# DMA transposes for the second parity's normalised rows, and attention units with scores and weighted values side by side

## The chip, the core and the metric

The kernel runs on one core of a Trainium2 chip. The metric is the device time of one execution in microseconds, of which medians of several executions are quoted. Each execution comes with the mean clock that was granted to TensorE, as a share of full speed. An execution is called slow when it lies more than 1.5% above the fastest one of the same kernel; the others, fast. Engine names in profile lines: PE is TensorE (matmuls), PEld its weight loads, DVE is VectorE, ACT is ScalarE, POOL is GpSimd, SPq is the queue of SyncE, which issues most DMAs.

## The reference, cut to what matters

```python
xn = layernorm(x)                       # x: 1 x 2048 x 512, bf16
# A: sliding attention, 32 heads of 16, window of 8 keys at distance 2
qkv = xn @ wqkv
s   = softmax(q . k[pos - 0, 2, ..., 14] * scale) @ v  @ wo
# B: MLP with shifted groups
h   = gelu(layernorm(xn) @ w1);  x1 = xn + shift(h) @ w2
g   = silu(x1 + gelu(layernorm(x1) @ w3) @ w4)
out = x + s * g
```

Keys stand at even distances, so even and odd rows never attend to each other. The kernel splits the 2048 rows by parity: chunks 0 and 1 (512 rows each) are the even rows, chunks 2 and 3 the odd ones, the "second parity".

## The kernel before

Each chunk of normalised rows is used transposed (in PE's profile lines `qk_ps<-xnT` and `w_ps<-xn2T`), once as it is (`xnT`, for queries, keys and values) and once normalised again, that is scaled by one factor per row (`xn2T`, for w1). Before the change PE transposes the rows with an identity matrix, a further matmul (`rrep_ps`) spreads the row factors over all partitions, and VectorE multiplies.

```python
def transposes(c, h):                 # h: half of the chunk, 8 PE transposes
    ...
    pin(nc.tensor.transpose(pt[:, dt, j, :], x_c[:, jj, dt * P : (dt + 1) * P], ident[:]))
    ...
    pin(nc.vector.tensor_copy(out=xnT[p][:, :, t0 : t0 + 2 * P], in_=...))

def rr_spread(c):
    ...                               # diagonal of row factors, on VectorE
    pin(nc.tensor.matmul(rp, lhsT=ones_bf[:], rhs=dg, start=True, stop=True))
    nc.scalar.activation(rrep, rp, AF.Copy)

def stage_b(c):                       # w2, residual, third layer norm
    ...
    pin(nc.sync.dma_start(out=x1n_dram[c * CH : (c + 1) * CH, :]..., in_=xn3))
    x1nT = sm4.tile([P, ND, CH], BF16, name="x1nT", tag="s4")
    pin(nc.sync.dma_start_transpose(out=x1nT, in_=x1n_dram[c * CH : (c + 1) * CH, :]))

def fill_mask(p, w):                  # 8 DMAs of 128 KB: mask rows next to each head's keys or queries
    t = (kT[p], qT[p])[w]
    for e in range(2):
        for gr in range(4):
            r = 32 * gr + DH * (1 - e)
            pin(nc.sync.dma_start(out=t[e][r : r + DH, :, :], in_=mask_d[w]....to_broadcast([DH, ND, M])))
```

`pin` keeps an engine's instructions in the order of the program. All pinned `nc.sync` DMAs therefore form one fixed list on SyncE. A stage is named after what it multiplies with (qk, w1, w3) or is stage B. The stages of the first half run in this order:

```python
for c in range(1, NCH):               # before the change
    if c + 1 < NCH: ln_stats(c + 1)
    stage_tr(c); stage_w1(c - 1); rr_spread(c); rr_mult(c)
    if c + 1 < NCH: ln_norm(c + 1); stage_qk(c)
    if c == 2: fill_mask(0, 0); fill_mask(0, 1)
    if c == 1: build_mask()           # rows computed on GpSimd, written to mask_d
stage_b(0); stage_w1(3); stage_b(1); stage_qk(3); stage_b(2)
stage_w3(0); stage_b(3); stage_w3(1); stage_w3(2); stage_w3(3)
```

The second half has 18 attention units. While ScalarE takes exponentials of one unit's scores, PE does pieces of the w4 and wo products ("fill" in the code, not to be confused with the mask fills):

```python
for n, (p, u) in enumerate(order):    # before the change
    prs = [scores(p, u, 0)]
    for f in fill[n][0]: f()
    prs.append(scores(p, u, 1))
    for f in fill[n][1]: f()
    if prev is not None: weighted(*prev)     # 32 matmuls, then VectorE empties the bank
    prev = (p, u, va, prs)
    if n + 1 < len(order): va = values(*order[n + 1])
    ...
```

The softmax here doesn't subtract the row's maximum and nothing guards it: scores larger than these inputs give would overflow.

Of the kernel before, what the change touches and what calls it, by code (L numbers as in the profile page):

```python
# [8 lines left out]
AF = mybir.ActivationFunctionType  # L9
# [6 lines left out]
def kernel(  # L16
# [62 lines left out]
    mask_d = dram.tile([2, 16, M], BF16, name="mask_d")  # L79
    x1n_dram = dram.tile([S, D], BF16, name="x1n_dram")  # L80

    def bigt(shape, name):
        return big.tile(shape, BF16, name=name, tag="big")

    def midt(shape, name):
        return mid.tile(shape, BF16, name=name, tag="s11")
# [30 lines left out]
    def pin(ins):  # L117

        prev = pinned.get(ins.ins.engine)
        if prev is not None:  # L120
            tc.add_manual_dep(
                ins.ins, prev, mybir.DependencyInfo(mybir.DependencyClass.NoSync, mybir.DependencyReason.DATA),
                reason="pinned",
            )
        pinned[ins.ins.engine] = ins.ins.name
        return tc.keep_in_program_order(ins)
# [4 lines left out]
    for c in range(NCH):  # L131
# [14 lines left out]
    nc.sync.dma_start(out=w2_sb, in_=B_w2.rearrange("(g q) n -> q g n", q=P))  # L146
    w3_sb = midt([P, ND, F], "w3_sb")
    nc.sync.dma_start(out=w3_sb, in_=B_w3.rearrange("(dt q) f -> q dt f", q=P))
    wv_sb = const.tile([P, ND, D], BF16, name="wv_sb")
    nc.sync.dma_start(out=wv_sb, in_=wqkv_v[:, :, 2 * D : 3 * D])  # L150
    w4_sb = midt([P, NF, D], "w4_sb")
    nc.sync.dma_start(
        out=w4_sb[:, 0 : NF - 1, :],
        in_=B_w4[0 : (NF - 1) * P, :].rearrange("(ft q) n -> q ft n", q=P),
    )
    nc.sync.dma_start(out=w4_sb[0:FL, NF - 1, :], in_=B_w4[(NF - 1) * P : F, :])
    nc.scalar.preload_act_table_set("gelu_apprx_tanh_and_others")


# [74 lines left out]
    def fill_mask(p, w):  # L234
# [3 lines that stand above are left out]
# [4 lines left out]
                    )  # L242
                )


    NV = 2
    v_aug = []
# [81 lines left out]
    def stage_tr(c):  # L329
        for h in range(TPC // 2):  # L330
            transposes(c, h)

    def rr_spread(c):
        p, k = c // 2, c % 2
# [133 lines left out]
    def w4_tile(c, jj, tag=None):  # L468

        p, i = c // 2, (c % 2) * TPC + jj  # L470
        st = {}

        def half(lo, hi):
            if lo == 0:
                st["pt"] = pst(tag or "w", "w4_ps")[:, 0, :]
            pt = st["pt"]
            for ft in range(lo, hi):
                fs = P if ft < NF - 1 else FL
                pin(
                    nc.tensor.matmul(  # L480
                        pt, lhsT=h3[c][:fs, ft, jj * P : (jj + 1) * P], rhs=w4_sb[:fs, ft, :],
                        start=(ft == 0), stop=(ft == NF - 1),
                    )
                )
            if hi == NF:
                x_i = xn[p][:, i, :]
                pin(nc.vector.tensor_tensor(out=x_i, in0=pt, in1=x_i, op=ALU.add))  # L487
                if tag is not None:
                    nc.scalar.activation(x_i, x_i, AF.Silu)
                else:  # L490
                    st["sig"] = fin.tile([P, D], BF16, name="sig", tag="f")
                    nc.scalar.activation(st["sig"], x_i, AF.Tanh, scale=0.5)

        def gate():

            x_i = xn[p][:, i, :]
            pin(
                nc.vector.scalar_tensor_tensor(
                    out=x_i, in0=st["sig"], scalar=1.0, in1=x_i, op0=ALU.add, op1=ALU.mult
                )  # L500
            )

        return half, gate


# [3 lines left out]
    def values(p, u):  # L509
        q0, nq, k0, nk = units[u]  # L510
        va = v_aug[cnt["v"] % NV]
        cnt["v"] += 1
        vp = pst("b", "v_ps")[:, 0, :]
        for dt in range(ND):
            pin(
                nc.tensor.matmul(  # L516
                    vp[:nk, :], lhsT=xnT[p][:, dt, k0 : k0 + nk], rhs=wv_sb[:, dt, :],
                    start=(dt == 0), stop=(dt == ND - 1),
                )
            )  # L520
        pin(nc.vector.tensor_copy(  # L521
            out=va[:nk, :, 0:DH], in_=vp[:nk, :].rearrange("p (h d) -> p h d", d=DH)
        ))
        return va

    def scores(p, u, dd):
        q0, nq, k0, nk = units[u]
        pr = sm4.tile([P, H * P // 2], BF16, name="prob", tag="s4")
        prv = pr[:, 0 : H * nq // 2].rearrange("p (r x) -> p r x", r=4)
        for h in range(2):  # L530
            st = pst("st"[h], "s_ps")
            for i in range(4):
                dt, e = 2 * dd + i // 2, i % 2
                for b in range(2):
                    r = 64 * h + 32 * b
                    pin(
                        nc.tensor.matmul(  # L537
                            st[:nk, b, i * nq : (i + 1) * nq], lhsT=kT[p][e][r : r + 32, dt, k0 : k0 + nk],
                            rhs=qT[p][e][r : r + 32, dt, q0 : q0 + nq], start=True, stop=True,
                            tile_position=(r, 0),  # L540
                        )
                    )
            with tc.issue_after(last["gelu"].ins):
                nc.scalar.activation(  # L544
                    prv[:nk, 2 * h : 2 * h + 2], st[:nk, :, 0 : 4 * nq], AF.Exp, scale=SCALE
                )
        return pr

    def weighted(p, u, va, prs, tag="o"):
        q0, nq, k0, nk = units[u]  # L550
        r = next(i for i, x in enumerate(runs[p]) if u < x[1])
        ra = runs[p][r][2]
        if u == runs[p][r][0]:
            rw = runs[p][r][3]
            orw[p] = orwp.tile([P, 2 * ND * RW], BF16, name="orw", tag="orw")[:, 0 : 2 * ND * rw].rearrange(
                "p (j s q) -> p j s q", j=2, s=ND
            )
        op = pst(tag, "o_ps")
        for jj in range(2):
            for dt in range(ND):  # L560
                for cg in range(4):
                    b, e = cg // 2, cg % 2
                    pi = jj * 8 + b * 4 + (dt % 2) * 2 + e
                    pin(
                        nc.tensor.matmul(  # L565
                            op[32 * cg : 32 * cg + 32, jj, dt * nq : (dt + 1) * nq],
                            lhsT=va[:nk, dt * 8 + 4 * jj + cg, :],
                            rhs=prs[dt // 2][:nk, pi * nq : (pi + 1) * nq],
                            start=True, stop=True, tile_position=(0, 32 * cg),
                        )  # L570
                    )
        pin(nc.vector.tensor_copy(  # L572
            out=orw[p][:, :, :, q0 - ra : q0 - ra + nq],
            in_=op[:, :, 0 : 4 * nq].rearrange("p j (s q) -> p j s q", q=nq),
        ))
        if u == runs[p][r][1] - 1:
            normalise(p, r)
# [136 lines left out]
    rr_mult(0)  # L714
    ln_norm(1)
    stage_qk(0, [1, 2, 3])
    for c in range(1, NCH):
        if c + 1 < NCH:
            ln_stats(c + 1)
        stage_tr(c)  # L720
        stage_w1(c - 1)
        rr_spread(c)
        rr_mult(c)
        if c + 1 < NCH:
            ln_norm(c + 1)
            stage_qk(c)
        if c == 2:
            fill_mask(0, 0)
            fill_mask(0, 1)
        if c == 1:  # L730
            build_mask()
    stage_b(0)
    stage_w1(3)
    stage_b(1)
# [16 lines left out]
    for n in range(2 * NU):  # L751
        if n < 10:
            t, a, b, c = n, 0, 8, NF
        elif n < 14:
            t, a, b, c = (n // 2 + 5, 0, 4, 5) if n % 2 == 0 else (n // 2 + 5, 5, 9, NF)
        else:
            t, (a, b, c) = NW - 1, ((0, 3, 3), (3, 6, 6), (6, 9, 9), (9, NF, NF))[n - 14]
        fill[n][0].append(lambda t=t, a=a, b=b: w4s[t][0](a, b))
        if c > b:
            fill[n][1].append(lambda t=t, b=b, c=c: w4s[t][0](b, c))  # L760
            if c == NF:
                fill[n + 1][0].append(w4s[t][1])
        if n >= 10:
            fill[n][0].append(lambda i=n - 10: final_tile(0, i))
        if n >= 12 and n % 2 == 0:
            fill[n][2].append(lambda i=n - 12: store(nc.sync, 0, i))
# [16 lines left out]
    for n, (p, u) in enumerate(order):  # L783
        prs = [scores(p, u, 0)]
        for f in fill[n][0]:
            f()
        prs.append(scores(p, u, 1))
        for f in fill[n][1]:
            f()
        if prev is not None:  # L790
            weighted(*prev)
        prev = (p, u, va, prs)
        if n + 1 < len(order):
            va = values(*order[n + 1])
        for f in fill[n][2]:
            f()
# [4 lines left out]
            ident.rearrange("k (h a) -> k a h", a=DH).unsqueeze(3).to_broadcast([P, DH, 8, DH]), AF.Copy,  # L801
        )
    )
    weighted(*prev, tag="s")
    final_tile(1, 0, tag="b")
    final_tile(1, 1, tag="o")
    w4s[NW - 1][1]()
# [48 lines left out]
```

## Time and profile before

| | before |
|---|---|
| median of the first 3 runs | 214.15 us (213.87 to 214.18) |
| span in the profile | 211.9 us |
| PE busy | 201.7 us, 95% |
| next busiest engine, ACT | 139.6 us, 66% |
| mean granted clock | 0.999 |

These are lines of the first page of the profile of the kernel before: busy time by engine, then PE's busy tenths, the granted clock and the DMA share in 40 equal slices of the span.

```profile
PE 201.7 (95%) x1978; PEld 96.5 (46%) x2007; DVE 131.0 (62%) x254; ACT 139.6 (66%) x160; POOL 55.5 (26%) x118
PE   8998999999999999999989999999999999998991
PEclk9999999999999999999999999999999999999999
DMA  5999314998240275599930003724325542445142
```

PE has no hole in its row: a digit of 8 or 9 in every slice but the last. So I took the time for the length of PE's list, and work taken off it for worth its full length unless something new makes PE wait: an estimate from this row, which e10 below bears out (1.5 to 2.6 us gained for 2.2 us taken off).

The next lines are PE's timeline before, in the columns start, length (us), engine, source line, operation, output and inputs, shapes and count. They are the transposes and replication matmuls of chunks 2 and 3, and the first matmuls that read stage B's transposed rows.

```profile
28.35 1.06 PE L321 MATMUL tr_ps<-ident,xn_96 128*128 128x128 bf16 x16
32.70 0.39 PE L348 MATMUL rrep_ps<-xn2T,ones_bf 128*128 128x512 bf16 x1
39.83 1.06 PE L321 MATMUL tr_ps<-ident,xn_96 128*128 128x128 bf16 x16
44.18 0.38 PE L348 MATMUL rrep_ps<-xn2T,ones_bf 128*128 128x512 bf16 x1
65.11 5.13 PE L458 MATMUL w_ps<-x1nT,w_sb 128*128 128x512 bf16 x23
```

From each start to the next matmul's start is 0.89, 0.23, 0.90 and 0.22 us: 2.2 us in all. The w3 stage starts at 65.11 and does not wait.

SyncE's list before, in the same columns (length is now the time to issue, not to land):

```profile
29.59 0.38 SPq L232 DMA_DIRECT2D mask_d<-m_rows_424  x1
35.46 1.74 SPq L240 DMA_DIRECT2D kT_151<-mask_d  x4
44.29 3.58 SPq L240 DMA_DIRECT2D qT_156<-mask_d  x4
55.02 0.40 SPq L436 DMA_DIRECT2D x1n_dram<-xn_662  x1
57.97 2.09 SPq L441 DMA_TRANSPOSE x1nT<-x1n_dram  x1
```

The mask fills are issued from 35.5 to 47.9 us (12.4 us) and, by the DMA share in windows of 1 us, their data flow from 37 to 52. Stage B's first write is issued at 55.0, when the fills are through. Its transpose follows 2.95 us later and lands about 4 us after that, some 3 us before PE needs it.

### The profile page before, as it was taken

Reading aid. Unit: us, or ns where it says so; the run is one execution under the profiler, and the core shown is the slowest. Engines: PE = TensorE matmul, PEld = TensorE weight load, DVE = VectorE, ACT = ScalarE, POOL = GpSimd, SP = SyncE. Lnnn points to the kernel's source line nnn. Section 1 sums busy time; section 2 is a strip of 40 time slices with the busy share of each in tenths; the row PEclk is TensorE's granted clock in tenths of the full one; section 3 lists DMA queues with packets and bytes.
Section 4 is the critical chain, followed back from the end, with each engine's and each line's share of the span. In section 5 each row is a group of like instructions: output and inputs, shape, how many; then the busy total and the mean of one; then the engine's idle time right before and its main releaser. Section 6 shows DMA issues by size and latency. Waiting matters only on the chain.

```text
span 211.9 us, 4839 instructions
## 1 busy us (share of the span) xinstructions
PE 201.7 (95%) x1978; PEld 96.5 (46%) x2007; DVE 131.0 (62%) x254; ACT 139.6 (66%) x160; POOL 55.5 (26%) x118
## 2 busy tenths in 40 slices
PE   8998999999999999999989999999999999998991
PEld 2544454544444444444444444444445544454440
DVE  6879396338839456000014666767767889688785
ACT  2098797943393625565599888788597888975310
POOL 4645774001120202000000008508039070253000
PEclk9999999999999999999999999999999999999999
DMA  5999314998240275599930003724325542445142
GB/s 152 375 395 389 117 8 6 147 145 108 99 99 3 99 198 99 140 174 126 120 39 3 0 3 61 216 80 76 114 82 141 168 103 33 129 121 107 31 147 99
DMA packets 30990, 25.16 MB, mean 119 GB/s; under 512 B 15960, under 2 KB 26424, under 8 KB 30968
## 3 DMA queue, kind: packets, MB, share of 16 engines
q1 hardware_dynamic: 27224, 19.02, 40.0%
q0 software_dynamic: 2192, 4.57, 9.1%
q10 hardware_dynamic: 1552, 1.27, 2.0%
q8 instruction: 16, 0.26, 0.6%
q14 instruction: 6, 0.05, 0.1%
HBM read 16.15 MB, written 4.37 MB: 97 GB/s over the span
## 4 chain that ended last, share of the span: by engine, by line
PE 80%; DVE 7%; DMA 5%; ACT 2%; issue 2%; POOL 1%; SPq 1%; DVEq 0%; ACTq 0%
PE w_ps L458 18%; PE w_ps L480 16%; PE qk_ps L372 10%; PE v_ps L516 7%; PE s_ps L537 7%; PE w_ps L421 6%; PE wo_ps L677 6%; PE w_ps L391 5%; PE o_ps L565 4%; DMA xn_95<-in_A_x_dram 3%; DMA oT_2427<-orw 2%; ACT prob L544 2%; DVE l1s_243 L284 1%; DVE l1s_299 L284 1%; DVE sg L686 1%
## 5 line engine op out<-in xcount | busy, mean ns | idle before, releaser
L544 ACT ACTIVATE prob<-s_ps 128x960 bf16<-128x960 f32 (+2 forms) x72 | 62.7, 925 | 11.6 <-PE s_ps L537 11.2
L480 PE MATMUL w_ps<-w_sb,h3T 128*128 128x512 bf16 (+1 forms) x174 | 43.6, 381 | 0.2 <-issue 0.2
L458 PE MATMUL w_ps<-x1nT,w_sb 128*128 128x512 bf16 (+1 forms) x173 | 38.2, 379 | 0.2
L464 ACT ACTIVATE h3T<-w_ps 128x1024 bf16<-128x1024 f32 x20 | 20.5, 1024 | 20.9 <-PE w_ps L458 20.9
L599 POOL DMA_DIRECT2D oT_1480<-orw x24 | 12.4, 525 | 61.3 <-DVE orw L572 61.3
L458 PEld LDWEIGHTS <-w_sb 128*128 128x128 bf16 (+1 forms) x176 | 17.6, 100 | 20.4
L480 PEld LDWEIGHTS <-h3T 128*128 128x128 bf16 (+1 forms) x176 | 14.7, 98 | 16.4
L521 DVE CAST v_aug_145<-v_ps 128x512 bf16<-128x512 f32 (+1 forms) x9 | 6.1, 681 | 23.1 <-PE v_ps L516 23.0
L572 DVE CAST orw<-o_ps 128x960 bf16<-128x960 f32 (+2 forms) x18 | 19.7, 1097 | 0.4 <-PE o_ps L565 0.4
L372 PEld LDWEIGHTS <-wqk_sb 128*128 128x128 bf16 x136 | 13.3, 98 | 14.3 <-issue 0.3
L599 POOL DMA_DIRECT2D oT_2427<-orw x20 | 10.1, 513 | 20.9 <-DVE orw L572 20.9
L487 DVE TENSOR_TENSOR xn_95<-w_ps,xn_95 128x512 bf16<-128x512 f32 x8 | 5.5, 692 | 16.0 <-PE w_ps L480 16.0
L372 PE MATMUL qk_ps<-xnT_149,wqk_sb 128*128 128x512 bf16 (+1 forms) x71 | 14.3, 355 | 0.3 <-DVE xnT_149 L324 0.2
L391 PE MATMUL w_ps<-xn2T,w_sb 128*128 128x512 bf16 x61 | 14.3, 379 | 0.2
L372 PE MATMUL qk_ps<-xnT_150,wqk_sb 128*128 128x512 bf16 x64 | 14.1, 379 | 0.0
L262 POOL TENSOR_SCALAR l3r<-l3m 128x4 f32<-128x4 f32 x4 | 1.0, 246 | 43.4 <-DVE l3m L270 43.4
L380 ACT ACTIVATE qT_155<-qk_ps 128x1024 bf16<-128x1024 f32 x4 | 4.1, 1030 | 9.8 <-PE qk_ps L372 9.8
L427 DVE TENSOR_TENSOR xn_96<-w_ps,xn_96 128x1024 bf16<-128x1024 f32 x4 | 4.9, 1216 | 8.3 <-PE w_ps L421 8.3
L421 PE MATMUL w_ps<-w_sb,hT_160 128*128 128x512 bf16 x32 | 9.5, 379 | 0.0
L516 PE MATMUL v_ps<-wv_sb,xnT_150 128*128 128x512 bf16 (+1 forms) x28 | 8.9, 383 | 0.4
L391 PEld LDWEIGHTS <-w_sb 128*128 128x128 bf16 x64 | 6.1, 98 | 6.8
L421 PE MATMUL w_ps<-w_sb,hT_159 128*128 128x512 bf16 x30 | 9.1, 379 | 0.1
(161 smaller groups left out, 328.8 us busy)
## 6 DMA issues: line engine op xcount, KB each, us to landing
w_sb<-in_B_w_dram SPq DMA_DIRECT2D x1, 1376.0 KB
w_sb<-in_B_w_dram SPq DMA_DIRECT2D x1, 1280.0 KB
wqk_sb<-in_A_wqkv_dram SPq DMA_DIRECT2D x2, 512.0 KB
w_sb<-in_B_w_dram SPq DMA_DIRECT2D x2, 512.0 KB
xn_96<-in_A_x_dram SPq DMA_DIRECT2D x4, 256.0 KB
xo_1598<-in_A_x_dram POOLq DMA_DIRECT2D x4, 256.0 KB, 3.9
xo_2228<-in_A_x_dram POOLq DMA_DIRECT2D x4, 256.0 KB, 3.7
out_dram<-xo_1598 SPq DMA_DIRECT2D x3, 256.0 KB
```

The costliest lines, as they stand in the source:

```text
L372: nc.tensor.matmul(pt[:, b, h : h + n], lhsT=wqk_sb[:, dt, nt * P : (nt + 1) * P], rhs=xnT[p][:, dt, k * CH + h : k * CH + h + n], start=( ...
L391: nc.tensor.matmul(pt[:, b, :], lhsT=w1_sb[:, dt, g * P : (g + 1) * P], rhs=xn2T[:, dt, :], start=(dt == 0), stop=(dt == ND - 1),)
L421: nc.tensor.matmul(pt[:, j, :], lhsT=w2_src(p, g, m0), rhs=w2_sb[:, g, :], start=(g == 0), stop=(g == ND - 1),)
L458: nc.tensor.matmul(pt[:fs, ft % 2, :], lhsT=w3_sb[:, dt, ft * P : ft * P + fs], rhs=x1nT[:, dt, :], start=(dt == 0), stop=(dt == ND - 1),)
L464: last["gelu"] = nc.scalar.activation(h3T[:, 2 * a : 2 * a + 2, :], pt, AF.Gelu_apprx_tanh)
L480: nc.tensor.matmul(pt, lhsT=h3[c][:fs, ft, jj * P : (jj + 1) * P], rhs=w4_sb[:fs, ft, :], start=(ft == 0), stop=(ft == NF - 1),)
L516: nc.tensor.matmul(vp[:nk, :], lhsT=xnT[p][:, dt, k0 : k0 + nk], rhs=wv_sb[:, dt, :], start=(dt == 0), stop=(dt == ND - 1),)
L537: nc.tensor.matmul(st[:nk, b, i * nq : (i + 1) * nq], lhsT=kT[p][e][r : r + 32, dt, k0 : k0 + nk], rhs=qT[p][e][r : r + 32, dt, q0 : q0 + ...
L544: nc.scalar.activation(prv[:nk, 2 * h : 2 * h + 2], st[:nk, :, 0 : 4 * nq], AF.Exp, scale=SCALE)
L572: pin(nc.vector.tensor_copy(out=orw[p][:, :, :, q0 - ra : q0 - ra + nq], in_=op[:, :, 0 : 4 * nq].rearrange("p j (s q) -> p j s q", q=nq),))
L599: (nc.scalar if (p, r) == (1, 2) and jj else nc.gpsimd).dma_start(out=oT[p][DH * hh : DH * (hh + 1), :, ra : ra + rw], in_=orw[p][32 * cg ...
L677: nc.tensor.matmul(pt, lhsT=oT[p][:, dt, i * P : (i + 1) * P], rhs=wo["sb"][:, dt, lo:hi], start=(dt == 0), stop=(dt == ND - 1),)
```

## The change

Chunks 2 and 3 are no longer transposed by PE. The rows and the scaled rows are written to DRAM and come back through two DMA transposes. To keep the DMA queues free for that, the loads of wv and w4 move behind chunk 2's transposes, and the mask is built behind chunk 3's. In the attention units the weighted values follow directly on the second scores, so that the form of the matmuls changes less often (128\*128, 32\*128 or 128\*32 in the profile lines), and w4 work of units 10 to 13 moves in front of the second scores. The exponentials are pinned to program order. The diff, cut to its core:

```diff
+    def late_loads():                     # wv and w4, until now loaded at the start
+        pin(nc.sync.dma_start(out=late["wv"], in_=wqkv_v[:, :, 2 * D : 3 * D]))
+        pin(nc.sync.dma_start(out=late["w4"][:, 0 : NF - 1, :], in_=B_w4...))
+        ...
+    def dma_tr(c):
+        pin(nc.sync.dma_start(out=xn_dram[0, cs, :]..., in_=x_c))
+        xn2 = sm4.tile([P, TPC, D], BF16, name="xn2", tag="s4")
+        for j in range(TPC):
+            pin(nc.vector.tensor_scalar(out=xn2[:, j, :], in0=x_c[:, j, :], scalar1=r2[:, j : j + 1], ...))
+        pin(nc.sync.dma_start(out=xn_dram[1, cs, :]..., in_=xn2))
+        pin(nc.sync.dma_start_transpose(out=xnT[p][:, :, cs], in_=xn_dram[0, cs, :]))
+        xn2Ts[c] = sm4.tile([P, ND, CH], BF16, name="xn2T", tag="s4")
+        pin(nc.sync.dma_start_transpose(out=xn2Ts[c], in_=xn_dram[1, cs, :]))
...
-    for c in range(1, NCH):  (the loop shown above)
+    ln_stats(2); stage_tr(1); stage_w1(0); rr_spread(1); ln_norm(2)
+    dma_tr(2)
+    late_loads()
+    rr_mult(1); stage_qk(1); ln_stats(3); ln_norm(3)
+    dma_tr(3)
+    build_mask()
+    stage_w1(1); stage_qk(2)
+    fill_mask(0, 0)
+    fill_mask(0, 1)
+    stage_w1(2)
     stage_b(0)
...
-            t, a, b, c = (n // 2 + 5, 0, 4, 5) if n % 2 == 0 else (n // 2 + 5, 5, 9, NF)
+            t, a, b, c = (n // 2 + 5, 0, 5, 5) if n % 2 == 0 else (n // 2 + 5, 5, NF, NF)
...
         prs.append(scores(p, u, 1))
+        if prev is not None:
+            op = weighted(*prev)
         for f in fill[n][1]:
             f()
         if prev is not None:
-            weighted(*prev)
+            keep(*prev[0:2], op)
```

More of the change, by code (lines that the diff above doesn't have):

```diff
@@ L80 @@
     x1n_dram = dram.tile([S, D], BF16, name="x1n_dram")
+    xn_dram = dram.tile([2, M, D], BF16, name="xn_dram")
     def bigt(shape, name):
@@ L148 @@
     nc.sync.dma_start(out=w3_sb, in_=B_w3.rearrange("(dt q) f -> q dt f", q=P))
-    wv_sb = const.tile([P, ND, D], BF16, name="wv_sb")
-    nc.sync.dma_start(out=wv_sb, in_=wqkv_v[:, :, 2 * D : 3 * D])
-    w4_sb = midt([P, NF, D], "w4_sb")
-    nc.sync.dma_start(
-        out=w4_sb[:, 0 : NF - 1, :],
-        in_=B_w4[0 : (NF - 1) * P, :].rearrange("(ft q) n -> q ft n", q=P),
-    )
-    nc.sync.dma_start(out=w4_sb[0:FL, NF - 1, :], in_=B_w4[(NF - 1) * P : F, :])
     nc.scalar.preload_act_table_set("gelu_apprx_tanh_and_others")
@@ L243, in fill_mask @@
                 )
+    late = {}
+    def late_loads():
+        late["wv"] = const.tile([P, ND, D], BF16, name="wv_sb")
+        pin(nc.sync.dma_start(out=late["wv"], in_=wqkv_v[:, :, 2 * D : 3 * D]))
+        late["w4"] = midt([P, NF, D], "w4_sb")
+        pin(
+            nc.sync.dma_start(
+                out=late["w4"][:, 0 : NF - 1, :],
+                in_=B_w4[0 : (NF - 1) * P, :].rearrange("(ft q) n -> q ft n", q=P),
+            )
+        )
+        pin(nc.sync.dma_start(out=late["w4"][0:FL, NF - 1, :], in_=B_w4[(NF - 1) * P : F, :]))
     NV = 2
@@ L331, in stage_tr @@
             transposes(c, h)
+    def dma_tr(c):
+        p, k = c // 2, c % 2
+        cs = slice(k * CH, (k + 1) * CH)
+        x_c = xn[p][:, k * TPC : (k + 1) * TPC, :]
+        pin(nc.sync.dma_start(out=xn_dram[0, cs, :].rearrange("(i q) d -> q i d", q=P), in_=x_c))
+        r2 = r2s.pop(c)
+        xn2 = sm4.tile([P, TPC, D], BF16, name="xn2", tag="s4")
+        for j in range(TPC):
+            pin(
+                nc.vector.tensor_scalar(
+                    out=xn2[:, j, :], in0=x_c[:, j, :], scalar1=r2[:, j : j + 1], scalar2=None, op0=ALU.mult
+                )
+            )
+        pin(nc.sync.dma_start(out=xn_dram[1, cs, :].rearrange("(i q) d -> q i d", q=P), in_=xn2))
+        pin(nc.sync.dma_start_transpose(out=xnT[p][:, :, cs], in_=xn_dram[0, cs, :]))
+        xn2Ts[c] = sm4.tile([P, ND, CH], BF16, name="xn2T", tag="s4")
+        pin(nc.sync.dma_start_transpose(out=xn2Ts[c], in_=xn_dram[1, cs, :]))
     def rr_spread(c):
@@ L480, in half @@
                     nc.tensor.matmul(
-                        pt, lhsT=h3[c][:fs, ft, jj * P : (jj + 1) * P], rhs=w4_sb[:fs, ft, :],
+                        pt, lhsT=h3[c][:fs, ft, jj * P : (jj + 1) * P], rhs=late["w4"][:fs, ft, :],
                         start=(ft == 0), stop=(ft == NF - 1),
@@ L491, in half @@
                     st["sig"] = fin.tile([P, D], BF16, name="sig", tag="f")
-                    nc.scalar.activation(st["sig"], x_i, AF.Tanh, scale=0.5)
+                    pin(nc.scalar.activation(st["sig"], x_i, AF.Tanh, scale=0.5))
         def gate():
@@ L516, in values @@
                 nc.tensor.matmul(
-                    vp[:nk, :], lhsT=xnT[p][:, dt, k0 : k0 + nk], rhs=wv_sb[:, dt, :],
+                    vp[:nk, :], lhsT=xnT[p][:, dt, k0 : k0 + nk], rhs=late["wv"][:, dt, :],
                     start=(dt == 0), stop=(dt == ND - 1),
@@ L543, in scores @@
             with tc.issue_after(last["gelu"].ins):
-                nc.scalar.activation(
+                pin(nc.scalar.activation(
                     prv[:nk, 2 * h : 2 * h + 2], st[:nk, :, 0 : 4 * nq], AF.Exp, scale=SCALE
-                )
+                ))
         return pr
@@ L551, in weighted @@
         r = next(i for i, x in enumerate(runs[p]) if u < x[1])
-        ra = runs[p][r][2]
         if u == runs[p][r][0]:
@@ L571, in weighted, with keep @@
                     )
+        return op
+    def keep(p, u, op):
+        q0, nq, k0, nk = units[u]
+        r = next(i for i, x in enumerate(runs[p]) if u < x[1])
+        ra = runs[p][r][2]
         pin(nc.vector.tensor_copy(
@@ L716 @@
     stage_qk(0, [1, 2, 3])
-    for c in range(1, NCH):
-        if c + 1 < NCH:
-            ln_stats(c + 1)
-        stage_tr(c)
-        stage_w1(c - 1)
-        rr_spread(c)
-        rr_mult(c)
-        if c + 1 < NCH:
-            ln_norm(c + 1)
-            stage_qk(c)
-        if c == 2:
-            fill_mask(0, 0)
-            fill_mask(0, 1)
-        if c == 1:
-            build_mask()
+    ln_stats(2)
+    stage_tr(1)
+    stage_w1(0)
+    rr_spread(1)
+    ln_norm(2)
+    dma_tr(2)
+    late_loads()
+    rr_mult(1)
+    stage_qk(1)
+    ln_stats(3)
+    ln_norm(3)
+    dma_tr(3)
+    build_mask()
+    stage_w1(1)
+    stage_qk(2)
+    fill_mask(0, 0)
+    fill_mask(0, 1)
+    stage_w1(2)
     stage_b(0)
@@ L758 @@
         fill[n][0].append(lambda t=t, a=a, b=b: w4s[t][0](a, b))
+        if b == NF and n < 14:
+            fill[n + 1][0].append(w4s[t][1])
         if c > b:
@@ L803 @@
     )
-    weighted(*prev, tag="s")
+    keep(*prev[0:2], weighted(*prev, tag="s"))
     final_tile(1, 0, tag="b")
```

## The prediction

The sum reads 214.15 - 2.2 - 1.3 + 7 = 217.65, about 218 us. The 1.3 us is my estimate from the 0.11 us of excess in the trace. The 7 us rests on the order of SyncE's list and on my estimate that the write's data come behind the fills'.

> **What bounds the kernel now.** The page's engine table has PE busy 201.7 of 211.9 us (95%), the next engine (ACT) 66%; the chain of waits is 80% PE. From 30 to 110 us PE is busy 9.3 to 10 of every 10. So time taken from PE's in-order list counts, and so does every wait put into it.
>
> **What is removed from PE.**
> (a) Sixteen transposes and one replication matmul for each of the two chunks of the second parity. In PE's timeline transposes take 28.35-29.24 and 39.83-40.73, replication matmuls 32.70-32.93 and 44.18-44.40: 2.2 us in all.
> (b) A steady attention unit takes 4.94 us in six blocks: scores 0.34, eight w4 matmuls 1.84, scores 0.51, three w4 0.75, weighted 0.53, values 0.97. A 512-column matmul costs 0.216, so each full-array block leaves about 0.11 us of excess where the array form changes. [...] Weighted next to scores makes five changes of six in some 13 units, though ACT (84% busy) limits the last four of them. I estimate 1.3 us.
> Together -3.5 us: without a new wait, 210.6 us.
>
> **What is added and moved.** SyncE's queue gets, in fixed order: two 512 KB writes and two transposes for chunk 2, the late weight loads (1.9 MB), the same four for chunk 3, mask rows, sixteen mask fills, and only then stage B's first write and transpose. [...] Durations from the trace: write to usable 2.4-2.9 us, transpose issue 2.1, landing about 4, mask rows to first fill 5.1-5.9, fills 12.4 to issue and about 16 to land, loads about 390 GB/s.
> - Chunk 2: normalised about 22.5 us, transposes landed by about 32. The plain one lands about 29.5, wanted at 31.8: no wait.
> - Chunk 3: normalised about 31; its writes queue behind the late loads (data until about 36), so its transposes issue at 38-43 and land by 45; wanted at 45.6: just in time.
> - Masks: rows cannot go before about 42, fills run about 47-64 (before: 35.5-52). The table's buffer may come later, giving 5 us more.
> - Stage B chunk 0: its write, ready at about 53, sits behind the fills until 60, its data behind theirs until 65; its transpose lands about 70. PE wants it for the first w3 stage at 65.1-2.2 = 62.9. **New wait of about 7 us (3 at best, 12 at worst), all critical.** Before, it landed 3 us early.
>
> Later stages shift whole; the second mask fill has 40 us of slack; the tail is unchanged.
>
> **Prediction:** 214.15 - 2.2 - 1.3 + 7 = about 218 us, slower. Range 209 to 223; the low end is the case in which the masks go out earlier and nothing waits. Chances: faster by over 2% 0.17, within 2% 0.25, slower 0.58.
>
> **What would show it.** Right: one PE gap of several us before the first matmul that reads the transposed x1n, released by a DMA; mask fills issued at about 47-60 and stage B's first write only then; attention units about 4.83 us. Wrong: first w3 matmul at about 63 without a gap; or a gap before a qk or w1 stage.
>
> **What would make it wrong.** Mask rows earlier than queue order suggests; faster fills; late loads delaying less; [...] ACT, now held in order, stalling the scores.

## The result, and the profile after

| | before | after |
|---|---|---|
| runs | 213.33 to 214.18 us | 226.47, 229.02 (fast), 230.54, 231.36 us (slow) |
| median | 214.01 us | 229.78 us |
| ratio of the fast runs | 1 | 1.065, interval 1.054 to 1.076 |
| mean granted clock | 0.999 | 0.969 in the fast runs, 0.93 in the profiled one |

Ratios here and below are the mean time of one kernel's fast runs over that of the other's of the same rounds, so they are not quite the ratio of the medians quoted.

The kernel after is slower. The profile is of a slow execution (231.36 us), so its total is not compared; the places of its two large gaps are the same in fast executions of the experiments below. The same four page lines, of the kernel after:

```profile
PE 204.8 (89%) x1944; PEld 96.0 (42%) x1973; DVE 127.5 (56%) x248; ACT 138.5 (60%) x158; POOL 55.1 (24%) x118
PE   8798999969970399999999999999999999998992
PEclk9999999999997579999999999999999999999999
DMA  6990799954995764028996000263542624342332
```

PE has fewer instructions (1944 instead of 1978) and is busy for less of the span. Its row now has two holes: a small one at a 6 (about 47 us) and one that reads 7, 0, 3. Under the second, the granted clock falls to 5.

PE's timeline after, at the two holes. The square brackets hold the idle time of PE just before, and what ended it:

```profile
49.14 3.76 PE L418 MATMUL w_ps<-xn2T,w_sb 128*128 128x512 bf16 x16 [1.76 <-DMA xn2T<-xn_dram]
78.06 1.44 PE L485 MATMUL w_ps<-x1nT,w_sb 128*128 128x512 bf16 x3 [10.76 <-DMA x1nT<-x1n_dram]
79.72 10.65 PE L485 MATMUL w_ps<-x1nT,w_sb 128*128 128x512 bf16 x40 [0.22 <-issue]
```

PE waits 1.76 us for chunk 3's scaled rows before a w1 stage and 10.76 us for stage B's first transposed rows before the first w3 stage. SyncE's list after tells why:

```profile
33.52 1.38 SPq L355 DMA_DIRECT2D xn_dram<-xn_448  x1
40.81 1.31 SPq L356 DMA_TRANSPOSE xnT_146<-xn_dram  x1
42.29 2.85 SPq L358 DMA_TRANSPOSE xn2T<-xn_dram  x1
47.91 0.37 SPq L226 DMA_DIRECT2D mask_d<-m_rows_467  x1
53.75 1.74 SPq L234 DMA_DIRECT2D kT_147<-mask_d  x4
62.78 2.84 SPq L234 DMA_DIRECT2D qT_152<-mask_d  x4
66.55 0.39 SPq L463 DMA_DIRECT2D x1n_dram<-xn_625  x1
73.58 1.70 SPq L468 DMA_TRANSPOSE x1nT<-x1n_dram  x1
```

Chunk 3's transposes are held until 40.8 us because its writes stand behind 1.9 MB of late loads (SyncE waits up to 5.9 us for such a write; with these loads moved away, in e6 below, the transposes went at 35.4 us). The mask rows, the fills and stage B's first write follow one after the other. That write's rows were ready on VectorE at 53.7 us (its last instruction of `xn_625`); it was issued at 66.55, and its transpose only 7.0 us after that, where before it took 2.95 us. In windows of 1 us the DMA share was still 1.05 to 1.12 from 67 to 71 us, which I read as the fills' data, with the write's behind them. The list of waits adds one more:

```profile
POOL m_tab L185 <- DMA xn_dram<-xn_448: 10.0, 1, 10.0
```

GpSimd waited 10.0 us to start the mask table, because the table shares a pool of five buffers with the new tiles and got the one that chunk 3's write held. Moving the table to an additional buffer of its own did not build: by the build's message the last pool needs 3 KB per partition and 2.8125 are left, so 192 bytes are missing.

The windows view of the kernel after (window, its length, busy time and count by engine, granted clock, DMA share, GB/s) shows what followed the second hole:

```profile
67.00:78.00 11.00, 0.29 (x2) 0.00 (x0) 6.41 (x17) 0.00 (x0) 1.36 (x2) 0.73 0.80 164
78.00:83.00 5.00, 4.72 (x11) 1.75 (x13) 0.00 (x0) 1.02 (x1) 0.00 (x0) 0.51 0.67 169
83.00:88.00 5.00, 5.00 (x24) 2.26 (x23) 0.00 (x0) 2.33 (x3) 0.00 (x0) 0.95 0.66 166
```

In the 5 us after the restart PE ran 11 matmuls where it ran 24 in the next 5. In windows of 1 us the clock was at 0.50 from 73 to 82 us: it fell 5.3 us after PE's last matmul and came back 4.8 us after the restart. From the means of these windows the fall is at 72.6 and the return at 82.9 us. In e2_tr below, worked out in the same way from windows of 5 and 10 us, the clock changed at about 49.4, 52.8, 73.3 and 83.6 us. The delays differ from run to run: in e5_own_tab the clock fell 2.7 us after the last matmul. A wait of 2.97 us (e7_gapfill) was enough. What sets the delays is not shown.

In this one profiled execution the clock was also 0.95 from 4 us on, before any gap. The profiled executions of the experiments below, on the same design, had 1.00 outside their gaps; what caused the 0.95 is open, and nothing below rests on that execution's total.

### The profile page after: what moved, and what is told of

It is laid out like the page before. It is cut to its first block, busy times and chain, and to the rows that moved or that the text cites. A ratio compares the mean times of both kernels' runs of the same rounds, so it can differ in the third digit from the quotient of the medians.

```text
span 229.6 us, 4784 instructions
## 1 busy us (share of the span) xinstructions
PE 204.8 (89%) x1944; PEld 96.0 (42%) x1973; DVE 127.5 (56%) x248; ACT 138.5 (60%) x158; POOL 55.1 (24%) x118
## 4 chain that ended last, share of the span: by engine, by line
PE 71%; DMA 11%; DVE 7%; ACT 6%; issue 2%; SPq 1%; POOL 1%; ACTq 0%
PE w_ps L485 18%; PE w_ps L507 17%; PE qk_ps L399 9%; PE s_ps L564 6%; ACT prob L571 6%; PE v_ps L543 5%; PE wo_ps L709 5%; PE w_ps L418 4%; PE w_ps L448 4%; DMA x1n_dram<-xn_625 3%; DMA xn2T<-xn_dram 3%; DMA xn_96<-in_A_x_dram 3%; PE o_ps L591 2%; DMA x1nT<-x1n_dram 2%; DVE sg L718 1%
## 5 line engine op out<-in xcount | busy, mean ns | idle before, releaser
L485 PE MATMUL w_ps<-x1nT,w_sb 128*128 128x512 bf16 (+1 forms) x173 | 41.8, 405 | 11.1 <-DMA x1nT<-x1n_dram 10.8
L507 PE MATMUL w_ps<-w_sb,h3T 128*128 128x512 bf16 (+1 forms) x164 | 42.0, 391 | 1.8 <-issue 1.7
L485 PEld LDWEIGHTS <-w_sb 128*128 128x128 bf16 (+1 forms) x176 | 18.4, 105 | 34.4 <-issue 14.5
L631 POOL DMA_DIRECT2D oT_1443<-orw x24 | 12.4, 525 | 63.2 <-issue 47.1
L418 PE MATMUL w_ps<-xn2T,w_sb 128*128 128x512 bf16 x61 | 14.9, 391 | 1.9 <-DMA xn2T<-xn_dram 1.8
L399 PE MATMUL qk_ps<-xnT_145,wqk_sb 128*128 128x512 bf16 (+1 forms) x71 | 14.8, 364 | 0.3 <-DVE xnT_145 L332 0.2
L399 PE MATMUL qk_ps<-xnT_146,wqk_sb 128*128 128x512 bf16 x63 | 14.7, 390 | 0.1
L448 PE MATMUL w_ps<-w_sb,hT_156 128*128 128x512 bf16 x32 | 9.9, 391 | 0.1
L448 PE MATMUL w_ps<-w_sb,hT_155 128*128 128x512 bf16 x31 | 9.6, 390 | 0.0
L543 PE MATMUL v_ps<-wv_sb,xnT_145 128*128 128x512 bf16 (+1 forms) x36 | 9.6, 390 | 0.0
```

The costliest lines, as they stand in the source:

```text
L399: nc.tensor.matmul(pt[:, b, h : h + n], lhsT=wqk_sb[:, dt, nt * P : (nt + 1) * P], rhs=xnT[p][:, dt, k * CH + h : k * CH + h + n], start=( ...
L418: nc.tensor.matmul(pt[:, b, :], lhsT=w1_sb[:, dt, g * P : (g + 1) * P], rhs=xn2T[:, dt, :], start=(dt == 0), stop=(dt == ND - 1),)
L448: nc.tensor.matmul(pt[:, j, :], lhsT=w2_src(p, g, m0), rhs=w2_sb[:, g, :], start=(g == 0), stop=(g == ND - 1),)
L485: nc.tensor.matmul(pt[:fs, ft % 2, :], lhsT=w3_sb[:, dt, ft * P : ft * P + fs], rhs=x1nT[:, dt, :], start=(dt == 0), stop=(dt == ND - 1),)
L507: nc.tensor.matmul(pt, lhsT=h3[c][:fs, ft, jj * P : (jj + 1) * P], rhs=late["w4"][:fs, ft, :], start=(ft == 0), stop=(ft == NF - 1),)
L543: nc.tensor.matmul(vp[:nk, :], lhsT=xnT[p][:, dt, k0 : k0 + nk], rhs=late["wv"][:, dt, :], start=(dt == 0), stop=(dt == ND - 1),)
```

## The experiments

The theory after the result: nothing is wrong with DMA transposes or with the units. SyncE's one list put the late loads ahead of chunk 3's transposes and the mask fills ahead of stage B's first write; PE waits for both (1.76 and 10.76 us in the profile of after), and after the longer wait its clock is at 0.50. Rivals: the attention half costs time; the granted clock is the main loss; DMA transposes are too slow or DMA lacks bandwidth.

### First call: the halves, and one move of the fills

**e1_attn** is the kernel before with the attention half of the diff alone.

> Attention half of the change alone, on the kernel before. Theory of the prediction (only the number of array-form changes counts): 214.1 - 1.3 = 212.8 us. Theory read from the trace of after: units 1 to 9 fall from 4.94 to about 4.72 us at full clock (-2.0 in all), but units 10 to 13 grow from about 4.55 to about 4.85 us, because all w4 work sits before the second scores and PE then waits for the exponentials (+1.3): net about -0.7, 213.4 us. Rival (the attention half is part of the loss): over 215 us.

Measured: 213.57 us median, ratio 0.997 (0.994 to 1.001). The lines below are PE's timeline of steady units, first of the kernel before, then of e1_attn (the scores between them are left out):

```profile
125.19 0.82 PE L480 MATMUL w_ps<-w_sb,h3T 128*128 128x512 bf16 x3
125.94 0.60 PE L565 MATMUL o_ps<-prob,v_aug_145 128*32 128x120 bf16 x32
126.47 1.04 PE L516 MATMUL v_ps<-wv_sb,xnT_149 128*128 128x512 bf16 x3
...
130.88 0.60 PE L565 MATMUL o_ps<-prob,v_aug_147 128*32 128x120 bf16 x32
```

```profile
125.05 0.60 PE L564 MATMUL o_ps<-prob,v_aug 128*32 128x120 bf16 x32
125.58 0.82 PE L480 MATMUL w_ps<-w_sb,h3T 128*128 128x512 bf16 x3
126.25 1.03 PE L516 MATMUL v_ps<-wv_sb,xnT 128*128 128x512 bf16 x4
...
129.88 0.60 PE L564 MATMUL o_ps<-prob,v_aug 128*32 128x120 bf16 x32
```

From one weighted block to the next it is 4.94 us before and 4.83 now: the one saved change of form is worth 0.10 to 0.11 us, as predicted. My reading of the trace of after (0.22 us a unit) was too high. But the first unit is 0.2 us longer (5.13 instead of 4.92 from values to values; it is 5.13 in e10 too, with the units of before, so the new order need not be the reason), and the last three units go from 4.13-4.19 to 4.30 us each. The net effect is not distinguishable from nothing.

**e3_attn_oldgroups** is e1_attn with the w4 work of units 10 to 13 divided as before:

```diff
-            t, a, b, c = (n // 2 + 5, 0, 5, 5) if n % 2 == 0 else (n // 2 + 5, 5, NF, NF)
+            t, a, b, c = (n // 2 + 5, 0, 4, 5) if n % 2 == 0 else (n // 2 + 5, 5, 9, NF)
```

> Attention half alone, but with the w4 work of units 10 to 13 divided as before (part of it after the second scores). If the regrouping costs the 1.3 us that the trace of after suggests: about 212.1 us, units 10 to 13 at about 4.4 us, and 1.3 us faster than the run with the regrouping. If the regrouping is harmless: equal to that run within 0.3 us.

Measured: 213.81 us, ratio 0.999 (0.995 to 1.003). The expectation failed: units 10 to 13 sum to 18.46 us instead of 18.92 in e1 (values to values; before: 18.43), but the time is not better. Counted from the first unit's values, PE is 0.54 us ahead of before at unit 13 and level with it at unit 17. The last units give it back.

**e2_tr** is the kernel after with the attention units of before: transposes, late loads and the new mask position alone.

> Transpose half alone (the kernel after with the attention units of before). Queue theory: same PE gap of about 10.8 us before the first w3 matmul and 1.8 us before a w1 stage, plus about 2.2 us of halved clock after the long gap, minus 2.2 us of PE work: 214.1 + 12.6 = about 226.7 us in a full-clock execution. Rival (the lower granted clock of the profiled run, or the attention half, makes a good part of the loss): clearly below 222 us here.

Measured: 229.49 us, ratio 1.068 (1.058 to 1.078), so the whole loss is in this half; the fast runs (227.1 to 230.1 us) are a little slower than the expected 226.7. Its profiled execution (228.86 us, fast, clock 1.00 outside the gaps) gives the ledger of the loss, from two lines of PE's timeline:

```profile
49.87 5.08 PE L418 MATMUL w_ps<-xn2T,w_sb 128*128 128x512 bf16 x16 [3.47 <-DMA xn2T<-xn_dram]
77.87 12.46 PE L485 MATMUL w_ps<-x1nT,w_sb 128*128 128x512 bf16 x44 [9.10 <-DMA x1nT<-x1n_dram]
```

PE waited 3.47 us before the w1 stage and 9.1 us before the first w3 stage. After each wait the clock was halved for a while: the w1 stage took 5.08 us where the same stage without a gap takes 3.62, and the first w3 stage 12.46 us where an undisturbed one takes 9.66. That is 3.5 + 9.1 + 1.5 + 2.8 = 16.9 us. Less the 2.2 us of PE work removed it is 14.7, against a span that is 227.1 - 211.9 = 15.2 us longer. The sum closes within half a microsecond.

**e4_fills_after_b0** is the kernel after with the fills behind stage B's first write and transpose:

```diff
     stage_qk(2)
-    fill_mask(0, 0)
-    fill_mask(0, 1)
     stage_w1(2)
     stage_b(0)
+    fill_mask(0, 0)
+    fill_mask(0, 1)
```

> The kernel after, with the sixteen mask fills of the first parity put behind stage B's first write and transpose in SyncE's order (two lines moved; the mask rows are needed only by the scores). Queue theory: the gap before the first w3 stage falls from 10.8 us to under 1 us, the clock does not drop to half, the w1 gap of 1.8 us stays, and a gap of at most 2 us may open before the second w3 stage, whose write now queues behind the fills: 213 to 215 us. Rival (the DMA transposes themselves or DMA bandwidth are too slow, not the queue order): gap stays above 6 us and time above 220 us.

Measured: 225.91 us, ratio 1.056 (1.052 to 1.060). The expectation of 213 to 215 us failed. PE's timeline of this run, the w3 stages:

```profile
66.29 9.66 PE L485 MATMUL w_ps<-x1nT,w_sb 128*128 128x512 bf16 x44
88.31 2.31 PE L485 MATMUL w_ps<-x1nT,w_sb 128*128 128x512 bf16 x5 [8.91 <-DMA x1nT<-x1n_dram]
```

The gap before the first w3 stage is gone, and a gap of 8.9 us stands before the second one. The fills, at work with stage B's traffic, now ran from 61.7 to about 81 us. Stage B's second write, issued at 74.7 behind them, was usable only at 84.0, 9.3 us later. So the order theory was right for the place of the gap, but I had taken the fills for shorter than they are: in both places tried, 16 to 20 us of fills made the next write that PE depends on late. By the numbers alone this run would have spoken for the rival; a free place for the fills was needed to decide.

### Second call: each suspect repaired, and the clock

**e5_own_tab** puts the mask table into a pool that is idle in this phase and holds its computation back until GpSimd's last row factors are done.

```diff
-        tab = sm4.tile([P, 3, P + 24], BF16, name="m_tab", tag="s4")
+        tab = fin.tile([P, 3, P + 24], BF16, name="m_tab", tag="f")
...
-    build_mask()
+    with tc.issue_after(last["pow"].ins):
+        build_mask()
```

> The kernel after, with the mask table in a buffer pool that stands idle in this phase, so that GpSimd builds the mask rows at about 33-39 us instead of waiting until 42.3 us for the write of chunk 3 to free a shared buffer. Queue theory: the rows can still not be written before SyncE has issued chunk 3's transposes (45 us), so they go at about 45 instead of 47.9 and the PE gap before the first w3 stage shrinks by about 2.7 us only, from 10.8 to about 8. Rival (the wait for the buffer is the main cause): the gap shrinks by 5 us or more. The w1 gap stays at about 1.8-2.7 us in both.

Measured: 228.49 us in one look; gap 12.6 us before the first w3 stage, 2.2 before w1. The rows were ready at 38.5 us, but SyncE was still issuing chunk 3's transposes and wrote them at 46.4 us, only 1.5 us earlier than in the kernel after. The gap did not shrink: stage B's write, issued at 65.8, was usable after 8.0 us this time, and PE, at full clock, arrived earlier than in the profile of after. So the buffer alone was not the main cause, as far as one look can show, and my expected 2.7 us did not appear either.

**e6_late_later** moves the late loads behind stage B's first transpose.

```diff
     dma_tr(2)
-    late_loads()
...
     stage_b(0)
+    late_loads()
```

> The kernel after, with the late loads of wv and w4 (1.9 MB) issued behind stage B's first transpose instead of ahead of chunk 3's writes. Queue theory: chunk 3's first write lands about 35 instead of 40.8 us, the w1 gap (1.8-3.5 us so far) disappears, the mask rows go about 5 us earlier, and the gap before the first w3 stage shrinks by about 5 us less what PE itself arrives earlier (2 us), to 6-8 us. Rival (the loads do no harm there; the writes are slow by themselves): w1 gap stays.

Measured: 222.80 us in one look. Chunk 3's transposes were issued at 35.4 instead of 40.8 us, the wait before w1 is gone, and the gap before w3 is 8.4 us, a little above the expected 6 to 8. The mask rows went at 42.9 us; the first fill followed 8.0 us later, not 5 to 6, for a reason that I did not find. The late loads thus cost the w1 wait and probably a part of the w3 gap (one look, and the gap varied between 9.1 and 12.6 us in e2 and e5).

**e7_gapfill** adds 46 matmuls to the kernel after, into a PSUM bank that nobody reads, ahead of the first w3 stage.

```diff
+    dummy = psb("dummy_ps")
+    for _ in range(46):
+        pin(nc.tensor.matmul(dummy, lhsT=ident[:], rhs=xnT[0][:, 0, 0:CH], start=True, stop=True))
     stage_w3(0)
```

> The kernel after, with 46 extra matmuls into an unread PSUM bank just before the first w3 stage (results unchanged): they only keep PE busy while it waits. If the granted clock falls to half because PE stood still for 11 us, it now stays full, w3's first matmuls run at 0.216 us instead of 0.43, and the run is 2 to 2.5 us faster than the kernel after (229.8 median before, its fast runs 226.5-229): 225 to 226 us with clock above 0.99 in an undisturbed run. Rival (the clock drop is unrelated to the gap): no gain, clock still below 0.98.

Measured: 227.32 us median, 225.02 to 228.27, ratio 1.061 (1.053 to 1.069). In its profile the first w3 stage took 9.66 us instead of 12.46 and the clock stayed at 1.00 there. The total was too scattered to show the gain: the intervals of this ratio and of the kernel after's overlap. It was repeated on a quieter kernel below.

**e8_nowait** puts the queue right: table as in e5, late loads as in e6, the query half of the fills behind stage B's last transpose, and the w4 work divided as before.

```diff
-    fill_mask(0, 1)
...
     stage_b(3)
+    fill_mask(0, 1)
```

> All of the change's transposes and side-by-side units, with the queue put right: mask table in the idle pool, late loads behind stage B's first transpose, the key half of the first parity's mask fills where the change has them, the query half behind stage B's last transpose, and w4 of units 10 to 13 divided as before. Queue theory: no PE gap over 0.7 us between 22 and 105 us, first w3 matmul at about 63 us, first scores at about 105 instead of 107.5: 214.1 - 2.2 (PE transposes) - 0.3 (attention, as measured alone) = 211.3 to 212 us. Rival (DMA transposes of these rows cost more than they save even with a free queue): over 214 us.

Measured: 210.89 us, 210.67 to 211.42, ratio 0.986 (0.983 to 0.989), outputs correct. That is 0.4 us below the expected 211.3 to 212 and faster than both kernels; the gain of 1.4% is clear of the noise. Its SyncE list and PE's two lines of the w3 stages:

```profile
39.10 1.71 SPq L226 DMA_DIRECT2D mask_d<-m_rows  x2
45.79 5.46 SPq L234 DMA_DIRECT2D kT<-mask_d  x8
58.03 1.72 SPq L469 DMA_TRANSPOSE x1nT<-x1n_dram  x1
86.68 4.31 SPq L234 DMA_DIRECT2D qT<-mask_d  x8
```

```profile
63.00 9.66 PE L485 MATMUL w_ps<-x1nT,w_sb 128*128 128x512 bf16 x44
75.95 28.65 PE L485 MATMUL w_ps<-x1nT,w_sb 128*128 128x512 bf16 x132
```

The transposed rows are issued at 58.0 us, and w3 starts at 63.00 without a wait, which is the 62.9 that the prediction had for a kernel without gaps. The second line is the three later w3 stages back to back. With the fills moved, DMA transposes of the same size arrive in time for every w3 stage; the rival falls.

### Third and fourth call: parts of the repaired kernel

**e9_nopins** is e3 without holding ScalarE's order.

```diff
-                pin(nc.scalar.activation(prv..., AF.Exp, scale=SCALE))
+                nc.scalar.activation(prv..., AF.Exp, scale=SCALE)
```

> Attention half alone on the kernel before, w4 work divided as before, and ScalarE's exponentials not held in program order. In the run with the order held, units 1 to 9 gained 0.10 us each but units 10 to 17 lost it again and the time was 0.999 of before. If holding ScalarE's order is what takes it back: units 14 to 17 return from 4.30 to about 4.19 us and the time is about 213.0 us. If the exponentials limit those units in any order: 213.5 to 213.9 us, the same as with the order held.

Measured: 213.67 us, ratio 1.0005 (0.999 to 1.002), the last three units still 4.30 to 4.44 us. The pins are not what takes the gain back. I believe that ScalarE sets the pace in these units, since its exponentials fill 3.67 of the 4.30 us; but it is idle for the other 0.63, so this is not shown, and why a unit becomes 4.30 instead of 4.19 us stays open.

**e10_tr_fixed** is e8 with the attention units of before.

> The repaired queue (mask table in the idle pool, late loads behind stage B's first transpose, query half of the fills behind its last) with the attention units of before: the transposes alone, without a wait. Theory: the whole gain of the repaired kernel (3.0 us) is the 2.2 us of PE transposes plus the 0.3 us of attention, so this one lies at 213.9 - 2.2 = 211.7 us or a little below, first w3 matmul at about 63.0 us. Rival (the side-by-side units are the larger part): over 212.7 us.

Measured: 211.68 us, ratio 0.9905 (0.988 to 0.993), first w3 matmul at 63.24. As expected: transposes with a free queue are worth the 2.2 us that they take off PE, within the interval (1.5 to 2.6 us of 213.6).

**e11_fixed_regroup** is e8 with the change's own division of w4 work, so the change as it is plus the repaired queue.

> The repaired queue with the change's own attention half, regrouping of units 10 to 13 included (the repaired kernel of the last call had the old division). Measured alone on the kernel before the two divisions differed by 0.2 us: expected 210.9 us within 0.4. If the regrouping helps or harms when the rest is early: outside of that.

Measured: 211.62 us, ratio 0.991 (0.989 to 0.993), a little above the expected 210.5 to 211.3. It is level with e10, so in the repaired kernel too the attention half as the change has it is worth nothing measurable. Whether the old division (e8, 0.986) is really half a per cent better was not settled; the two ran in different calls.

**e12_fills_in_front** is e8 with one repair undone: all sixteen fills ahead of stage B's first write.

```diff
     fill_mask(0, 0)
+    fill_mask(0, 1)
...
     stage_b(3)
-    fill_mask(0, 1)
```

> The repaired kernel with one of its repairs undone: all sixteen fills stand where the change puts them, ahead of stage B's first write; table buffer and late loads stay repaired. Queue theory: rows at 39, fills issued 46-58, stage B's write at about 58.5, usable at 65, transposed x1n at about 69.5 against PE's 63.0: one gap of 6 to 7 us and a clock at half for about 4 us of restart, 210.9 + 6.5 + 2 = 219 to 220 us. Rival (once table and loads are repaired, the fills no longer matter): within 1 us of the repaired kernel's 210.9.

Measured: 221.13 us, 220.60 to 221.71, ratio 1.035 (1.033 to 1.037). One gap of 7.68 us before the first w3 stage, and that stage took 11.52 us instead of 9.66. So the place of eight 128 KB fills makes 10.2 us (221.13 - 210.89), of which 7.7 + 1.9 = 9.6 are seen on PE. Stage B's write was issued at 58.75, as expected, and usable 7.65 us later, about 1 us more than expected; gap and time therefore lie a little above the expected 6 to 7 and 219 to 220 us. Undoing the other two repairs one at a time was not run.

**e13_front_gapfill** is e12 with 30 unread matmuls in the gap.

> The kernel with the fills in front (220.6 to 221.7 us, gap 7.7 us, first w3 stage 11.52 us instead of 9.66), plus 30 matmuls into an unread bank ahead of the first w3 stage (6.5 us of work inside the gap). If PE's standing still is what halves the clock, the first w3 stage takes 9.7 us, the clock stays at 1.00, the moment of arrival of the transposed x1n does not move, and the run is 1.9 us faster: about 219.2 us, ratio to before about 1.026 against 1.035. If the halving has another cause: 221 us and a stage of 11.5 us.

Measured: 218.46 us, ratio 1.022 (1.018 to 1.026). PE's timeline of e12, then of e13:

```profile
71.03 11.52 PE L485 MATMUL w_ps<-x1nT,w_sb 128*128 128x512 bf16 x44 [7.68 <-DMA x1nT<-x1n_dram]
```

```profile
63.36 6.64 PE L775 MATMUL dummy_ps<-xnT,ident 128*128 128x512 bf16 x29
70.92 9.66 PE L485 MATMUL w_ps<-x1nT,w_sb 128*128 128x512 bf16 x43 [0.93 <-DMA x1nT<-x1n_dram]
```

The rows arrive at the same time (71.0 and 70.9 us), the stage takes 9.66 again (mean clock of the profiled execution 0.999, in e12 0.983), and the kernel that does 30 useless matmuls is 1.3% faster. Here it was standing still that halved the clock, and these matmuls kept it up. The stage accounts for 1.9 us of the 2.7 (221.13 - 218.46; the two ran in different calls, each against before); the rest is not explained.

## Why the prediction was wrong in size

The direction and the mechanism were right: data late behind one queue, one long gap before the first w3 stage. The size was not. The step that failed is the size of the term "New wait of about 7 us (3 at best, 12 at worst)", and with it the sum, which had no other wait and no term for the clock. With e2's fast execution, PE waited 3.5 + 9.1 = 12.6 us instead of 7, and the halved clock after these waits cost another 4.3 us. The wait came out larger because the chain in front of it started late: in the profile of after the mask rows went at 47.9 us and not at 42, so stage B's write was issued at 66.5 and not at 60, and its transposed rows arrived at 78.1 and not at 70. The gap before a w1 stage is also one of the signs that the prediction itself had named as "Wrong". Point by point, in the prediction's words:

- "Sixteen transposes and one replication matmul ... 2.2 us in all": right. e10 gained 1.5 to 2.6 us, and the w3 stage starts at 63.0 to 63.2 us.
- "I estimate 1.3 us" for the units: mis-sized. The 0.11 us a unit is right, but the whole half gained 0.3 us between the medians, with an interval that includes zero. The last units give back most of it.
- "Chunk 3: ... land by 45; wanted at 45.6: just in time": this step failed. Its transposes were issued from 40.8 instead of 38 us, and the second had landed only at about 49.1, when PE's wait ended, instead of 45. PE waited 1.8 us in the profile of after, 2.2 to 3.5 in the runs at full clock. A plan with 0.6 us of slack behind 1.9 MB of loads is a plan to wait.
- "Masks: rows cannot go before about 42 ... the table's buffer may come later, giving 5 us more": they went at 47.9. The buffer did come late, but e5 shows that without it the rows go at 46.4: the longer issue of the transposes held SyncE as well (3.9 us for the second one in e5; 2.1 to 2.2 us for stage B's in the kernel before).
- "New wait of about 7 us (3 at best, 12 at worst)": 10.8 us in after, 9.1 in e2, 12.6 in e5. The larger part is the late issue of stage B's write, at 66.5 (68.1 in e2) and not at 60. A smaller part is its delay until it is usable: I had about 5 us behind the fills; it was 5.3 to 8.0 in the runs with all fills in front. PE itself came later too, at 67.3 instead of 62.9 us, which hid 4.4 us of the delay in the profile of after.
- Not in the prediction at all: the clock. It fell to half after the gap, which made the first w3 stage 1.6 to 2.8 us longer, and in two traces (waits of 3.0 and 3.5 us before w1) that stage took 1.5 to 1.7 us longer too. After waits of 2.2 and 2.7 us it did not. e13 shows the cause, in the kernel with the fills in front.

Added up, with waits and clock from the fast execution of e2: predicted waits 7, measured 12.6 us; predicted clock loss 0, measured 4.3 us; predicted gain of the units 1.3, measured 0.3 (from e1, since e2 has the units of before). These three differences (5.6 + 4.3 + 1.0 = 10.9 us) are the way from 218 to about 229; the fast runs of the kernel after were 226.5 and 229.0 us.

## What to carry to other kernels

Moving work from the busiest engine to DMA also moves it into a list whose order is fixed, here by `pin` on SyncE. List what stands behind each new transfer in that queue, with its data time, and find the first item behind it that the busy engine waits for; here the new transfers pushed 16 us of mask fills, which the scores needed only some 50 us later, in front of a write that was needed at once. With the table and the late loads repaired, moving half of those fills turned a loss of 3.5% into a gain of 1.4%. When a gap on PE cannot be avoided, count it as the gap plus a restart at half clock if it is long: in these traces the clock was halved after waits of 3.0 us and more, and the stage behind took 1.5 to 2.8 us longer; after waits of 1.8 to 2.7 us it was not.

## Costs measured in these runs

- One gap of 7.7 us in a PE that is otherwise busy cost 1.9 us more in the stage behind it (e12), and filling it with useless matmuls gained 2.7 of 221 us (e13).
- The execution profiled for the kernel after had a granted clock of 0.95 from 4 us on, outside of its gap, in a program on one core; the cause is open.
- Saving one change of form of six in a unit saved 0.10 to 0.11 us (e1).
- For a DMA transpose of 512 x 512 bf16 the issue held SyncE for 1.3 to 4.0 us, mostly 1.7 to 2.5. Stage B's transposes had landed 4.3 to 4.8 us after the issue began where PE waited for them; the second of chunk 3's two took 6.0 to 7.1 us. Alone, in the kernel before, the data flowed for about 3 us, at 120 to 220 GB/s.
- A write of 512 KB was usable about 2.9 us after its issue when alone (kernel before), but 5.3 to 9.3 us behind mask fills on the same queue (5.3 in e2, 9.3 in e4). The sixteen fills, each into 16 partitions, moved about 110 to 200 GB/s with the DMA engines shown as fully busy (kernel before from 39 to 51 us, e4 from 64 to 79 us, in windows of 1 us), the loads into 128 partitions 370 to 420 (kernel before, 14 to 22 us); whether the partitions are the reason was not tested.
